# Issuing the loads of q, k and v three to four slots ahead, in a chunked retention and bilinear FFN kernel

## The chip, the cores and the metric

The kernel runs on one core of one Trainium2 chip. The metric is device time in microseconds (us) of one execution. A time is given as the median of several runs; a profile is of a single execution, which has a time of its own.

## The reference, cut to what matters

The attention part is a recurrence over 768 tokens for 4 batches and 8 heads of width 64; its output, as 3072 rows of 512, goes through a bilinear feed-forward layer.

```python
gamma = 1.0 - 2.0 ** (-5.0 - np.arange(H))
for t in range(S):
    state = gamma * state + einsum('bhd,bhe->bhde', k[:, :, t], v[:, :, t])
    y[:, :, t] = scale * einsum('bhd,bhde->bhe', q[:, :, t], state)
x = y.transpose(0, 2, 1, 3).reshape(B * S, H * D)      # 3072 x 512
out = ((x @ w_a) * (x @ w_b)) @ w_out                  # 512 -> 1536 -> 512
```

q, k and v are float32 in device memory, laid out as batch, head, token, width. The output is float32, 3072 by 512.

## The kernel before

**Slots.** The 3072 tokens are cut into 24 slots of 128 tokens; slot t is chunk t mod 6 of batch t div 6. The first six slots have a path of their own (`casts2`, `flip2`, `scores2`). The change concerns slots 6 to 23.

**The way of one slot.** Slots go in pairs, an even slot and the odd one after it. (1) *Load*: `load_slot` (line 106) issues from SyncE (SP) one transfer of 256 KB for k and one for v of each slot, and `load_two` (line 126) one of 512 KB for q of the whole pair. They fill float32 buffers `kf`, `qf`, `vf`, one for a pair, of which the pool `raw` has three each (line 58). A row of k or v is 64 floats, so a transfer of k or v is made of pieces of 256 bytes; q takes two tokens a piece, 512 bytes. (2) *Casts*: `casts(t)` (line 290) multiplies k and q by the decay tables into the bf16 tile `kqb` (two operations on GpSimd, POOL), and casts v into `vb`, on POOL too, but for slots 12 to 19, whose cast `v_cast` runs on ScalarE (ACT). (3) *Flip*: `flip(t)` (line 300) issues from SP a DMA transpose of `kqb` into the slot's half of the pair's `kqT`. (4) *Turn*: `turn(new, old)` (line 392) puts a pair's work on TensorE (PE): the state update from `kqb` and `vb`, then the scores of both slots (`scores`, line 325, which read both halves of `kqT`), and later the two parts of the output `y`, which ACT copies into `xt`.

**The feed-forward part.** Groups of slots J (`TILES`) run `ffn_a` and `ffn_g` (lines 517, 531) for 12 column blocks, VectorE (DVE) multiplying the two into `ht`. The output product (`Group`, line 620) is a seven-product scheme: its left operands are sums of blocks of `ht`, called `hs` (`hsum`, line 599), made on DVE or POOL. For J = 3, `hsum(3, 3, ...)` and two rounds of `hsums(3, ...)` are put on POOL between `casts(14)`, `casts(15)` and `casts(16)`. The last group of eight slots (`big`, line 851) uses such a scheme for the first two products too, with weight sums `wsa`, `wsb` that POOL makes (`weight_pieces`, line 736), after which POOL also multiplies some `ht` blocks there.

**What sets the order.** The helper `seq` (line 95) chains every instruction to the one before it on its engine, so each engine runs its work in the order in which the Python program writes it. This holds for SP too: all loads, transposes and stores are issued by SP, one after the other, onto one hardware DMA queue, and an SP instruction that waits holds up everything after it. `casts(t)` ends with the flip of slot t and then the loads of slot t + 2 (lines 296 to 298); `casts_two(6)` does slots 6 and 7 at once and then loads slots 8 and 9 (line 315). The list `LOADS` (line 21) gives the loads issued early, the last of which, "s6", is slots 6 and 7. `LATE_Q` (line 20) holds q of the pairs 14 and 18 back until the odd slot's loads.

The program order on POOL of the stretch that matters: casts of 6 and 7, 8, 9, 10, 11, `hs` of J = 2 around casts of 12 and 13, casts of 14, `hs`, casts of 15, `hs`, 16, 17, `hs`, 18, `hs`, 19, 20, 21, six weight pieces, 22, 23. On PE the turns that take in a new pair are, in order, those of pairs 6, 8, 10, 12, 14, 16, 18, 20 and 22.

Of the kernel before, what the change touches and what calls it, by code (L numbers as in the profile page):

```python
# [16 lines left out]
PAIRS = 3  # L17


LATE_Q = {14, 18}  # L20
LOADS = "p0 p1 w0 w1 a1 b1 a2 k2 q2 b2 v2 o0 o1 o2 o3 o4 o5 s6".split()


@with_exitstack
def kernel(
# [19 lines left out]
    NSLOT = B * NCH  # L45
# [49 lines left out]
    def seq(bi):  # L95
        ins = bi.ins
        prev = last.get(ins.engine)
        if prev is not None:
            tc.add_manual_dep(ins, prev.name, nosync, reason="program order")
        last[ins.engine] = ins  # L100
        return bi
# [3 lines left out]

    def load_slot(t, names="kqv"):
        b, ci = divmod(t, NCH)
        if t - 1 in LATE_Q:
            load_two("q", q, b, ci // 2, t - 1)
        for nm in names:  # L110
            src = {"k": k, "q": q, "v": v}[nm]
            if nm == "q":
                if t % 2 == 0 and t not in LATE_Q:
                    load_two(nm, src, b, ci // 2, t)
                continue
            if t % 2 == 0:
                whole[nm] = raw.tile([P, 2, H, D], F32, tag=nm + "f", name=nm + "f")
            raws[nm, t] = whole[nm][:, t % 2]
            s = src[b, :, ci * P : (ci + 1) * P, :].rearrange("h p d -> p h d")
            seq(nc.sync.dma_start(out=raws[nm, t], in_=s))  # L120

    def load_slots(t):
        for u, names in ((t, "kq"), (t + 1, "k"), (t, "v"), (t + 1, "v")):
            load_slot(u, names)

    def load_two(nm, src, b, u, t):
        f = raw.tile([P, H, 2, D], F32, tag=nm + "f", name=nm + "f")
        s = src[b, :, 2 * u * P : 2 * (u + 1) * P, :].rearrange("h (p two) d -> p h two d", two=2)
        seq(nc.sync.dma_start(out=f, in_=s))  # L129
        for par in range(2):  # L130
            raws[nm, t + par] = f[:, :, par, :]
# [25 lines left out]

    pending = list(LOADS)

# [78 lines left out]
    def cast(engine, dst, src):  # L238
        if engine is nc.scalar:
            seq(nc.scalar.copy(dst, src))  # L240
        else:
            seq(engine.tensor_copy(dst, src))  # L242
# [29 lines left out]
    def scaled(eng, t, i):  # L272
        tab = tabs[0] if i else tabs[1 if t < 2 * PAIRS else 2]
        dst, src, tab = kqb[t][:, i], raws["kq"[i], t], tab[:, t % NCH]
        if t < 2 * PAIRS:
            dst, src = (x.rearrange("p (hp r) d -> p hp r d", r=2) if x is src else x
                        for x in (dst, src))
            tab = tab.rearrange("p (hp r) o -> p hp r o", r=2).to_broadcast([P, HP, 2, D])
        else:
            dst = dst.rearrange("p hp r d -> p r hp d")  # L280
            src = src.rearrange("p (r hp) d -> p r hp d", r=2)
            tab = tab.rearrange("p (r hp) o -> p r hp o", r=2).to_broadcast([P, 2, HP, D])
        seq(eng.tensor_tensor(dst, src, tab, op=ALU.mult))  # L283

    def new_nat(t):
        kqb[t] = nat.tile([P, 2, HP, 2, D], BF16, tag="kqb", name="kqb")
        kb[t], qb[t] = kqb[t][:, 0], kqb[t][:, 1]
        vb[t] = nat.tile([P, H, D], BF16, tag="vb", name="vb")

    def casts(t):  # L290
        new_nat(t)
        scaled(nc.gpsimd, t, 0)
        scaled(nc.gpsimd, t, 1)
        if t not in range(12, 20):
            cast(nc.gpsimd, vb[t], raws["v", t])
        flip(t)
        if t + 2 < NSLOT:
            load_slot(t + 2)

    def flip(t):  # L300
        if t % 2 == 0:
            kqT[t // 2] = tra.tile([P, 2, 2, HP, P], BF16, tag="kqT", name="kqT", bufs=3)
        seq(nc.sync.dma_start_transpose(
            out=kqT[t // 2][:, t % 2].rearrange("p a b c -> p (a b) c"),
            in_=kqb[t].rearrange("p a hp r d -> p (a hp r d)")))

    def casts_two(t):
        for u in (t, t + 1):
            new_nat(u)
            scaled(nc.gpsimd, u, 0)  # L310
            scaled(nc.gpsimd, u, 1)
            flip(u)
        for u in (t, t + 1):
            cast(nc.gpsimd, vb[u], raws["v", u])
        load_slots(t + 2)

    def half(i):
        return slice(64 * i, 64 * i + 64)
# [660 lines left out]
    for ft in range(NFT):  # L979
        ffn_ab(1, ft)  # L980
    casts_two(6)
    ffn_out(0, 0, 0)
    weight_sum(3)
# [4 lines left out]
    ffn_out(0, 1, 1)  # L988
    weight_sum(4)
    casts(8)  # L990
    ffn_out(0, 2, 0)
    ffn_out(0, 2, 1)
# [3 lines left out]
    ffn_out(0, 3, 0)  # L996
    ffn_out(0, 3, 1)
    casts(9)
    turn(None, 6)
    single(1, AT0, AT1, FF)  # L1000
    casts(10)
    casts(11)
    blocks(2, 3, 6)
# [98 lines left out]
```

## Time and profile before

| | us |
|---|---|
| median of 3 runs | 222.13 (222.07 to 222.4) |
| the profiled execution | 222.79 |
| its span, first to last instruction of the program | 221.1 |
| DVE busy | 138.0 |
| ACT busy | 99.3 |
| POOL busy | 141.2 |

The DMA queue that SP feeds (q1 on the page) had packets for 75.8% of the time of 16 DMA engines. The page lists 18 transfers of k, 18 of v at 256 KB each and 12 of q at 512 KB as the large groups of loads; 18 DMA transposes took a median of 4.2 us from issue to landing.

How to read it: the profiled execution took 222.79 us, 1.7 us more than its span, which lie around the program's instructions, and 0.66 us more than the median of the runs. Busy time of an engine says nothing of where it waits; the timelines of the engines, in us from the span's start, and the view of waits (who waited for whom, in total, times, longest) tell that. In a timeline a row is: start, duration, engine, line, operation, output and inputs, shapes, count, and in brackets the idle time of the engine before it and what ended it. SPq is SP's queue of DMA issues; a row of it is the time for which SP was busy issuing, not the transfer, whose landing another view gives.

### The profile page before, as it was taken

How to read it: one execution, taken by the hardware profiler on the slowest of the kernel's cores; microseconds unless marked ns; L12 is line 12 of the kernel's file. 1: busy time of each engine (PE TensorE's matmuls, PEld its weight loads, DVE VectorE, ACT ScalarE, POOL GpSimd, SP SyncE). 2: the span in 40 equal slices, each digit the busy share in tenths (PEclk: the TensorE clock that was granted, in tenths of full speed). 3: DMA queues.
4: the chain of work that ended last, by engine and by line, in shares of the span. 5: the costliest groups of instructions: out<-in, count | busy, mean ns of one | idle time of the engine just before them, and what ended most of it. 6: DMA issues, size and time to landing. Idle time of an engine off the chain costs nothing.

```text
span 221.1 us, 5640 instructions
## 1 busy us (share of the span) xinstructions
PE 212.3 (96%) x2242; PEld 143.3 (65%) x2242; DVE 138.0 (62%) x254; ACT 99.3 (45%) x217; POOL 141.2 (64%) x163
## 2 busy tenths in 40 slices
PE   6789999999999999998999999999999999999994
PEld 2467445687468888887888565456865444448883
DVE  3776356846393463774377246986595777789642
ACT  3255325342243453453475345445545656542331
POOL 5265876775364659349782976999999996520000
PEclk9999999999999999999999999999999999999999
DMA  6999999998999999869999999990022000000054
GB/s 167 290 323 367 382 313 361 374 235 152 251 193 291 207 236 220 180 143 190 271 181 247 225 147 227 246 175 3 4 80 110 0 1 3 0 0 1 27 190 166
DMA packets 85146, 39.68 MB, mean 179 GB/s; under 512 B 57472, under 2 KB 78848, under 8 KB 85120
## 3 DMA queue, kind: packets, MB, share of 16 engines
q1 hardware_dynamic: 84976, 39.26, 75.8%
q8 instruction: 17, 0.28, 0.6%
q10 hardware_dynamic: 144, 0.07, 0.1%
q14 instruction: 9, 0.07, 0.1%
HBM read 28.31 MB, written 6.29 MB: 157 GB/s over the span
## 4 chain that ended last, share of the span: by engine, by line
PE 87%; SPq 4%; DMA 4%; POOL 2%; issue 1%; DVE 1%; ACT 0%; DVEq 0%
PE a L525 19%; PE g L537 18%; PE mA L641 12%; PE uA L781 8%; PE mB L641 6%; PE o L562 5%; PE uB L781 4%; DMA wstb<-in_moe_w_b_dram 4%; SPq L129 3%; PE mC L641 3%; PE at L330 2%; PE y L378 2%; PE uC L781 2%; PE st L348 2%; POOL hs L575 2%; PE ka L840 2%
## 5 line engine op out<-in xcount | busy, mean ns | idle before, releaser
L539 DVE TENSOR_TENSOR ht<-g,asb 128x256 bf16<-128x256 f32 (+1 forms) x74 | 36.9, 502 | 38.4 <-PE g L537 33.8
L525 PE MATMUL a<-xt,wa_bf 128*128 128x256 bf16 (+1 forms) x296 | 52.4, 305 | 0.2
L537 PE MATMUL g<-xt,wb_bf 128*128 128x256 bf16 (+1 forms) x296 | 52.2, 304 | 0.2 <-POOL wb_bf L242 0.2
L528 ACT CAST asb<-a 128x256 bf16<-128x256 f32 (+1 forms) x74 | 32.3, 437 | 39.0 <-PE a L525 36.6
L537 PEld LDWEIGHTS <-wb_bf 128*128 128x128 bf16 x296 | 28.6, 98 | 12.8 <-POOL wb_bf L242 0.3
L525 PEld LDWEIGHTS <-wa_bf 128*128 128x128 bf16 x296 | 27.9, 98 | 12.5 <-POOL wa_bf L242 0.4
L283 POOL TENSOR_TENSOR kqb<-kf,ktab 128x512 bf16<-128x512 f32 x22 | 23.0, 1051 | 16.6 <-DMA kf<-in_k_dram 14.9
L283 POOL TENSOR_TENSOR kqb<-qf,qtab 128x512 bf16<-128x512 f32 x18 | 19.0, 1053 | 12.8 <-DMA qf<-in_q_dram 12.8
L641 PEld LDWEIGHTS <-hs 128*128 128x128 bf16 x240 | 23.1, 98 | 5.6 <-POOL hs L575 1.7
L787 ACT COPY snap<-uA 128x512 f32<-128x512 f32 x30 | 16.7, 588 | 13.1 <-PE uA L781 13.1
L336 DVE TENSOR_TENSOR aT<-at,mask 128x512 bf16<-128x512 f32 x36 | 22.3, 681 | 0.3
L648 ACT COPY snaps<-mA 128x256 f32<-128x256 f32 x30 | 11.2, 374 | 21.2 <-PE mA L641 21.2
L641 PEld LDWEIGHTS <-ht 128*128 128x128 bf16 x180 | 17.5, 98 | 2.8
L575 POOL TENSOR_TENSOR hs<-ht,hs 128x384 bf16<-128x384 bf16 (+1 forms) x17 | 16.5, 982 | 2.5 <-DVE ht L539 2.5
L641 PE MATMUL mA<-wsum,hs 128*128 128x256 bf16 x120 | 16.1, 273 | 1.1 <-POOL hs L575 1.1
L575 POOL TENSOR_TENSOR ht<-gsb,asb 128x512 bf16<-128x512 bf16 x12 | 13.5, 1159 | 4.5 <-DVE gsb L575 4.5
L242 POOL CAST vb<-vf 128x512 bf16<-128x512 f32 x16 | 10.1, 645 | 8.4 <-DMA vf<-in_v_dram 8.2
L575 DVE TENSOR_TENSOR osb<-mB,snaps 128x256 f32<-128x256 f32 x20 | 8.4, 422 | 9.1 <-PE mB L641 4.7
L575 POOL TENSOR_TENSOR hs<-ht 128x384 bf16<-128x384 bf16 (+2 forms) x12 | 13.8, 1153 | 0.0
L389 ACT CAST xt<-y 128x512 bf16<-128x512 f32 x18 | 9.7, 589 | 2.3 <-PE y L378 2.2
L562 PE MATMUL o<-wo_bf,ht 128*128 128x512 bf16 x48 | 10.7, 379 | 0.0
L575 DVE TENSOR_TENSOR gsb<-uB,snap 128x512 bf16<-128x512 f32 x10 | 6.9, 685 | 5.4 <-ACT snap L787 2.6
(104 smaller groups left out, 325.9 us busy)
## 6 DMA issues: line engine op xcount, KB each, us to landing
qf<-in_q_dram SPq DMA_DIRECT2D x12, 512.0 KB, 5.9
out_dram<-osb SPq DMA_DIRECT2D x21, 256.0 KB, 4.2
kf<-in_k_dram SPq DMA_DIRECT2D x18, 256.0 KB, 4.6
vf<-in_v_dram SPq DMA_DIRECT2D x18, 256.0 KB, 5.3
wsta<-in_moe_w_a_dram SPq DMA_DIRECT2D x6, 512.0 KB, 7.9
wstb<-in_moe_w_b_dram SPq DMA_DIRECT2D x6, 512.0 KB, 8.2
wsto<-in_moe_w_out_dram SPq DMA_DIRECT2D x6, 512.0 KB, 8.7
kf<-in_k_dram SPq DMA_DIRECT2D x3, 512.0 KB, 7.2
```

Of the source, the lines that this page charges most:

```text
L283: seq(eng.tensor_tensor(dst, src, tab, op=ALU.mult))
L336: seq(nc.vector.tensor_tensor(aT[t][:, r], at[r], mask.to_broadcast([P, HP, P]), op=ALU.mult))
L525: seq(nc.tensor.matmul(a, wa_bf[:, kt, fs], xcols(J, kt, c0, c1), start=(kt == 0), stop=(kt == KT - 1)))
L528: seq(nc.scalar.copy(asb, a))
L537: seq(nc.tensor.matmul(g, wb_bf[:, kt, fs], xcols(J, kt, c0, c1), start=(kt == 0), stop=(kt == KT - 1)))
L539: seq(nc.vector.tensor_tensor(ht[J][:, ft, c0:c1], g, asbs.pop((J, ft, c0)), op=ALU.mult))
L562: seq(nc.tensor.matmul(o, ht[J][:, ft, i * P : (i + 1) * P], wo_bf[:, ft], start=(ft == 0), stop=(ft == NFT - 1), skip_group_check=True))
L575: seq(eng.tensor_tensor(dst, x, y, op=op))
L641: seq(nc.tensor.matmul(m, w, right[:, j], start=(first and j == 0), stop=(j == NP - 1), skip_group_check=True))
L648: seq(nc.scalar.copy(self.snaps[:, n], self.bank["A"]))
L781: seq(nc.tensor.matmul(m, w, right[:, k], start=(first and k == 0), stop=(k == 1), skip_group_check=True))
L787: seq(nc.scalar.copy(self.snaps[n], self.bank["A"]))
```

## The change

Loads move ahead. The pair 8 is loaded right after the pair 6, ahead of the transposes of 6 and 7. After that the loads that follow a flip are those of a slot four later in place of two, up to slot 17. The loads of 18 and 19 follow the flip of 15, those of 20 and 21 the flip of 18, those of 22 and 23 the flip of 19. q of a pair always goes with its even slot, so `LATE_Q` is gone.

```diff
-LATE_Q = {14, 18}
-LOADS = "p0 p1 w0 w1 a1 b1 a2 k2 q2 b2 v2 o0 o1 o2 o3 o4 o5 s6".split()
+LOADS = "p0 p1 w0 w1 a1 b1 a2 k2 q2 b2 v2 o0 o1 o2 o3 o4 o5 s6 s8".split()
+AHEAD = {8: (12,), 9: (13,), 10: (14,), 11: (15,), 12: (16,), 13: (17,), 15: (18, 19),
+         18: (20, 21), 19: (22, 23)}
 def load_slot(t, names="kqv"):
     b, ci = divmod(t, NCH)
-    if t - 1 in LATE_Q:
-        load_two("q", q, b, ci // 2, t - 1)
...
-            if t % 2 == 0 and t not in LATE_Q:
+            if t % 2 == 0:
 def casts(t):
...
-        if t + 2 < NSLOT:
-            load_slot(t + 2)
+        for u in AHEAD.get(t, ()):
+            load_slot(u)
 def casts_two(t):
...
-        load_slots(t + 2)
+        load_slots(t + 4)
```

The instructions of PE, DVE, ACT and POOL and their order are the same in both kernels. Only the order of SP's queue differs; the same transfers are in it. With k, q, v for the parts of a pair's loads, T for a transpose and "out" for a store of 256 KB, SP's queue from the loads of pair 6 to the transpose of slot 13 is:

```
before: k6 q6 k7 v6 v7 | T6 T7 k8 q8 k9 v8 v9 out T8 k10 q10 v10 out out T9 k11 v11 out T10
        k12 q12 v12 T11 k13 v13 out out T12 k14 v14 T13 | q14 k15 v15 T14 ...
after:  k6 q6 k7 v6 v7 | k8 q8 k9 v8 v9 T6 T7 k10 q10 k11 v10 v11 out T8 k12 q12 v12 out out T9
        k13 v13 out T10 k14 q14 v14 T11 k15 v15 out out T12 k16 q16 v16 T13 | k17 v17 T14 ...
```

(q8 holds q of slots 8 and 9, and so on.)

## The prediction

> **What bounds the kernel now.** First the page: busy times, slices, the chain.
>
> ```profile
> span 221.1 us, 5640 instructions
> PE 212.3 (96%) x2242; PEld 143.3 (65%) x2242; DVE 138.0 (62%) x254; ACT 99.3 (45%) x217; POOL 141.2 (64%) x163
> ...
> DMA  6999999998999999869999999990022000000054
> ...
> PE 87%; SPq 4%; DMA 4%; POOL 2%; issue 1%; DVE 1%; ACT 0%; DVEq 0%
> ```
>
> PE sets the time: 96% busy and 87% of the chain that ended last. A load that lands earlier is worth only the PE idle time that it takes away. But the DMA row is at 9 almost as long as slots are loaded, up to slice 27 (149 us), so loads, transposes and stores compete there.
>
> Next the view of waits: POOL's with the loads, then PE's own with engines that this change can reach.
>
> ```profile
> POOL kqb L283 <- DMA kf<-in_k_dram: 14.9, 9, 3.8
> POOL kqb L283 <- DMA qf<-in_q_dram: 12.8, 5, 5.6
> ...
> PE mA L641 <- POOL hs L575: 1.1, 1, 1.1
> ```
>
> POOL waits 27.7 us for k and q; PE waits for POOL's sums 1.1 us, once. The reader is to see the ratio: most of POOL's waiting reaches nobody. The timelines of PE and PEld place these waits, and give the times at which PE first reads the transposes of a pair (L330, `scores`):
>
> ```profile
> 60.97 0.64 PE L330 MATMUL at<-kqT 64*64 64x128 bf16 x32
> ...
> 76.36 0.64 PE L330 MATMUL at<-kqT 64*64 64x128 bf16 x32
> ...
> 97.54 0.64 PE L330 MATMUL at<-kqT 64*64 64x128 bf16 x32
> ...
> 105.26 0.50 PE L641 MATMUL mA<-wsum,hs 128*128 128x256 bf16 x3 [1.07 <-POOL hs L575]
> 124.98 0.22 PEld L641 LDWEIGHTS <-hs 128*128 128x128 bf16 x3 [0.31 <-POOL hs L575]
> 179.44 0.59 PE L781 MATMUL uB<-xs,wsa 128*128 128x512 bf16 x2 [0.30 <-DVE asb L575]
> ```
>
> **What the change can take away.** Rows of POOL's timeline, then two of DVE's:
>
> ```profile
> 97.08 1.04 POOL L283 TENSOR_TENSOR kqb<-qf,qtab 128x512 bf16<-128x512 f32 x1 [5.58 <-DMA qf<-in_q_dram]
> 103.42 1.78 POOL L575 TENSOR_TENSOR hs<-ht,hs 128x384 bf16<-128x384 bf16 x2
> 120.41 1.04 POOL L283 TENSOR_TENSOR kqb<-qf,qtab 128x512 bf16<-128x512 f32 x1 [5.06 <-DMA qf<-in_q_dram]
> 134.47 1.04 POOL L283 TENSOR_TENSOR kqb<-kf,ktab 128x512 bf16<-128x512 f32 x1 [3.25 <-DMA kf<-in_k_dram]
> ...
> 101.13 0.42 DVE L539 TENSOR_TENSOR ht<-g,asb 128x256 bf16<-128x256 f32 x1 [0.30 <-PE g L537]
> 178.09 0.69 DVE L575 TENSOR_TENSOR gsb<-uB,snap 128x512 bf16<-128x512 f32 x1 [2.11 <-POOL ht L575]
> ```
>
> - The stall at 105.26. POOL stands still 5.58 us for q of 14, then runs without a gap and ends the `hs` that PE wants at 105.2 (103.42 + 1.78), where PE wanted it at 104.19 (105.26 - 1.07). With q14 issued ahead of T11 it is there in time. The last `ht` block which that `hs` reads is ready at 101.55 (101.13 + 0.42); one operation of 0.9 us (half of 1.78) then ends near 102.5, 1.7 us ahead of need. The stall goes: **1.1 us**.
> - The weight load at 124.98 waits 0.31 for the next such sum, behind the wait of 5.06 us for q of 18. That goes too: **0.2 us** (bounds 0 and 0.31, since weight loads partly overlap PE).
> - The wait of 3.25 us at 134.47 goes, since k21 now follows T18 and not T19. POOL then comes up to 3 us sooner to the `ht` product for which DVE waits 2.11 us at 178.09, and PE at 179.44: **0.3 us** (bounds 0 and 0.3).
>
> Sum of the gain: **1.6 us**, bounds 1.1 and 1.7. What is late next on PE without these is not POOL; it is what PE reads from DMA.
>
> **What it adds: work ahead of the transposes.** No transfer is added, but each T that PE waits for now has more of them in front of it in SP's one queue. From issue to landing, three transposes before (T7, T9, T13, one instruction each):
>
> ```profile
> L303 SPq DMA_TRANSPOSE kqT<-kqb x1: 1233/1233/1233, 52.3 to 52.3; - x1
> DMA to landing us min/median/max: 3.2/3.2/3.2
> ...
> L303 SPq DMA_TRANSPOSE kqT<-kqb x1: 2133/2133/2133, 66.9 to 66.9; - x1
> DMA to landing us min/median/max: 5.0/5.0/5.0
> ...
> L303 SPq DMA_TRANSPOSE kqT<-kqb x1: 1237/1237/1237, 89.6 to 89.6; - x1
> DMA to landing us min/median/max: 3.1/3.1/3.1
> ```
>
> They land at 55.5, 71.9 and 92.7: 5.5, 4.5 and 4.8 us before PE reads them (60.97, 76.36, 97.54). The second has loads and stores in flight before it and takes 1.8 us longer than the other two: a transpose stands behind what was issued before. [...]
>
> What the queue moves, by windows (the last two numbers are DMA share and GB/s):
>
> ```profile
> 52.30:57.00 4.70, 4.70 (x27) 2.37 (x26) 4.25 (x10) 0.96 (x2) 1.05 (x2) 1.00 0.83 159
> 57.00:85.30 28.30, 28.30 (x344) 21.45 (x343) 14.62 (x30) 11.17 (x27) 17.52 (x19) 1.00 1.22 240
> 85.30:92.70 7.40, 7.40 (x102) 6.34 (x101) 3.82 (x10) 2.96 (x8) 5.28 (x6) 1.00 0.84 169
> 74.60:76.00 1.40, 1.40 (x15) 1.18 (x12) 0.79 (x2) 0.59 (x2) 1.40 (x2) 1.00 1.23 37
> ```
>
> From 57.0 to 85.3 it was full, at 240 GB/s over all kinds of transfer. In the stretches around it ran at 159 and 169, so 1.6 us of 4.7 (1 - 159/240) and 2.2 us of 7.4 lay open. The row at 74.6 is a hold in a transpose: share 1.23 but 37 GB/s for 1.4 us; I take one such hold of 1.2 us more as the upper case for each of T9 and T13, none as the lower.
>
> - **T7** gets the five loads of pair 8 in front: 1.5 MB (4 x 256 KB + 512 KB) or 1.57 million bytes, 6.5 us at 240 GB/s, less the 1.6 us open: 55.5 + 4.9 = 60.4, in time for 60.97 (60.4 to 62.0 if the gap can't be filled). No cost.
> - **T9** gets k11, v11, k12, q12, v12 more, the same bytes: 71.9 + 6.5 - 1.6 = 76.8, or 78.0 with a hold. PE wants it at 76.36: 0.4 to 1.6 late.
> - **T13** gets k15, v15, k16, v16 and, two at 512 KB, q14 and q16: 2.10 million bytes, 8.7 us, less 3.8 open: 92.7 + 4.9 = 97.6, or 98.8 with a hold, against 97.54: 0.1 to 1.3 late; 2.3 more if the second opening isn't filled.
>
> PE runs in order, so a late T stops all of PE. Behind the scores stand the turn and the feed-forward blocks; nothing else fills the hole. Lateness doesn't add up, since a stop at T9 moves the need for T13 back too: the cost is the larger of the two. The middles are 1.0 and 0.7; I take **1.5 us**, since the larger of two uncertain numbers lies above either middle, and since both sums count on openings that are filled to the last; bounds 0 and 3.6. After T13 the need is looser: the next turn came at 112 us, and POOL, which keeps its lead, no longer holds SP.
>
> Other edits come at nothing. The buffers: the third of each is free, since the pair three before has been cast when the load's turn comes; for v of 18, 20, 22 ACT casts it (`v_cast`) before the flip that SP must pass anyway. Merging q of 14 and 18 with the even slot moves 512 KB each and is in the sums. If a buffer's wait did show, it would hold SP's queue with the same price as a late T.
>
> **The sum**, against the profiled execution (222.79, span 221.1 and 1.7 around it): 222.79 - 1.6 + 1.5 = 222.7. The median of the runs is 0.66 lower, 222.13, so the forecast on that scale is **222.0**: no change that can be told, since 0.2% (0.44 us) is about what a measurement of this kernel tells apart.
>
> **The rivals.**
>
> - *Transposes in time, faster.* If the queue fills its open 3.8 us and no hold falls on T9 or T13, the lateness is 0.4 or less and the gain stays: 222.13 - 1.6 + 0.2 = 220.7. For it: the shares of 0.83 and 0.84 show room. Against: the need is met to within tenths in two places. [...]
> - *Transposes later than the gain, slower.* The place is T13 (and T9 before it) at the head of a turn on PE; the price is each us of lateness one to one; it decides the sign from a lateness of 1.6 us. With both holds, or the second opening unfilled, T13 is 1.3 to 3.6 late, middle 2.7: 222.13 - 1.6 + 2.7 = 223.2. For it: share 1.22 over 28 us, and the hold in the row at 74.6. Against: after 85.3 the queue did have room.
> - *The stall stays.* If `hs` came late for another reason than q14, the cost stands without the gain: 222.13 + 1.5 = 223.6. Against it: POOL has no other gap before 103.42, and `ht` is ready at 101.55.
>
> **How the numbers follow.** Lateness decides: from 1.2 to 2.1 us with a gain of 1.6 is the forecast, within 0.2% either way (221.7 to 222.6); below it is the first rival, above it the second. Forecast 0.29; faster rival 0.31; slower rival 0.36; the stall stays 0.04. So faster 0.31, same 0.29, slower 0.40. Cases of both signs hold most of the chance, so the range spans them: from no lateness at all, 220.5 (222.13 - 1.6), to lateness 3.4, 223.9 (222.13 - 1.6 + 3.4), a little inside the upper bound of 3.6.
>
> **What would show it.** In the changed kernel POOL's rows after 80 us have no wait for q or k above 0.5 us, and the 1.07 us before `mA` at 105 is gone (else the gain is wrong). T13 takes 5 us or more from issue to landing and PE shows idle time before L330, released by the DMA of `kqT`, near 76 or 98 us (else the added cost is wrong). The DMA row stays full without a dip from slice 10 to slice 17. The forecast fails if idle time turns up before L330 near 61 us, or if SP waits for a buffer.

## The result, and the profile after

The changed kernel is **slower**: 223.81 us (median of 22 runs, 222.43 to 225.47) against 222.65 us for the kernel before on the same chip (22 runs, 221.81 to 223.94). The ratio is 1.0057, with an interval of 1.0034 to 1.0079. On the scale of the 222.13 us shown ahead of the prediction that is 223.4 us: the forecast of no change was wrong, the second rival (transposes later than the gain, 223.2) was right. The profiled execution took 224.07 us with a span of 222.4; before it was 222.79 and 221.1.

The page of the changed kernel, the same lines as before:

```profile
span 222.4 us, 5629 instructions
PE 212.2 (95%) x2231; PEld 143.7 (65%) x2242; DVE 139.5 (63%) x254; ACT 99.3 (45%) x217; POOL 141.6 (64%) x163
...
DMA  6999999999999999999998969900013000000054
...
PE 70%; DMA 14%; POOL 6%; SPq 4%; issue 2%; DVE 2%; ACT 0%; POOLq 0%; ACTq 0%
```

PE is as busy as before, so the 1.3 us that the span grew are idle time of PE. The DMA row has lost the dips that it had in the 10th, 17th and 18th slice, shows two new ones further on (the 22nd and 24th), and is done with the loads a slice sooner (a 0 in the 27th): the queue is filled earlier. And in the chain that ended last PE fell from 87 to 70%, while DMA rose from 4 to 14%: the chain now runs over the transposes and the loads in front of them.

The waits of POOL, then of PE (engine, line waited for: us in total, times, longest):

```profile
POOL kqb L282 <- DMA qf<-in_q_dram: 2.9, 3, 1.6
POOL kqb L282 <- DMA kf<-in_k_dram: 2.7, 4, 1.2
```

```profile
core 0 of [0], span 222.4 us
PE at L329 <- DMA kqT<-kqb: 3.0, 2, 1.8
```

POOL's 27.7 us of waiting for k and q are down to 5.6. In their place PE waits 3.0 us for transposes, where it waited for none before. PE's timeline shows where (line numbers are one lower in this kernel; L329 is the scores):

```profile
61.02 0.64 PE L329 MATMUL at<-kqT 64*64 64x128 bf16 x32
...
78.26 0.64 PE L329 MATMUL at<-kqT 64*64 64x128 bf16 x32 [1.79 <-DMA kqT<-kqb]
...
100.67 0.64 PE L329 MATMUL at<-kqT 64*64 64x128 bf16 x32 [1.22 <-DMA kqT<-kqb]
...
106.83 0.82 PE L640 MATMUL mA<-wsum,hs 128*128 128x256 bf16 x6
```

The six `mA` products that the stall of 1.07 us split into 3 and 3 (the second three at 105.26) run in one row; the waits of 0.31 and 0.30 us at 125 and 179 are gone too. But the scores of pairs 8 and 12 wait 1.79 and 1.22 us for the transposes T9 and T13. From issue to landing these two took:

```profile
L302 SPq DMA_TRANSPOSE kqT<-kqb x1: 1379/1379/1379, 72.3 to 72.3; - x1
DMA to landing us min/median/max: 5.9/5.9/5.9
...
L302 SPq DMA_TRANSPOSE kqT<-kqb x1: 4926/4926/4926, 93.5 to 93.5; - x1
DMA to landing us min/median/max: 7.1/7.1/7.1
```

T9 lands at 78.2 (before 71.9), T13 at 100.6 (before 92.7). Part of the delay lies ahead of the issue. POOL has the casts of slot 9 done at 65.9, but SP, still issuing the loads and stores in front, issues T9 at 72.3 (before 66.9). T13 is issued at 93.5 (before 89.6), when SP and the casts come free together. The windows of the changed kernel, last two numbers DMA share and GB/s, tell why:

```profile
52.30:57.00 4.70, 4.65 (x26) 2.39 (x26) 4.25 (x7) 0.96 (x2) 3.14 (x4) 1.00 1.10 239
57.00:85.30 28.30, 26.45 (x326) 19.81 (x326) 16.69 (x32) 10.79 (x26) 13.86 (x16) 1.00 1.18 233
85.30:92.70 7.40, 7.40 (x69) 6.39 (x67) 2.55 (x6) 2.92 (x8) 7.40 (x9) 1.00 1.22 230
92.70:100.60 7.90, 6.66 (x97) 5.50 (x96) 5.41 (x12) 3.69 (x10) 4.50 (x5) 1.00 1.24 191
97.40:99.40 2.00, 2.00 (x25) 1.58 (x22) 0.94 (x3) 1.27 (x4) 2.00 (x3) 1.00 0.93 19
75.60:77.00 1.40, 0.86 (x14) 0.50 (x12) 0.70 (x2) 0.74 (x2) 0.98 (x1) 1.00 1.14 43
```

Both openings are filled (239 for 159, 230 for 169 GB/s), as the prediction assumed. But the queue was held for 2.0 us at 19 GB/s up to 1.2 us before T13 landed, and for 1.4 us at 43 GB/s up to 1.2 us before T9 did.

### The profile page after: what moved, and what is told of

It is laid out like the page before. It is cut to its first block, busy times and chain, and to the rows that moved or that the text cites. A ratio compares the mean times of both kernels' runs of the same rounds, so it can differ in the third digit from the quotient of the medians.

```text
span 222.4 us, 5629 instructions
## 1 busy us (share of the span) xinstructions
PE 212.2 (95%) x2231; PEld 143.7 (65%) x2242; DVE 139.5 (63%) x254; ACT 99.3 (45%) x217; POOL 141.6 (64%) x163
## 4 chain that ended last, share of the span: by engine, by line
PE 70%; DMA 14%; POOL 6%; SPq 4%; issue 2%; DVE 2%; ACT 0%; POOLq 0%; ACTq 0%
PE a L524 12%; PE g L536 12%; PE mA L640 10%; PE uA L780 8%; DMA kqT<-kqb 6%; PE mB L640 5%; DMA qf<-in_q_dram 5%; PE o L561 5%; POOL kqb L282 4%; PE uB L780 4%; DMA wstb<-in_moe_w_b_dram 4%; SPq L128 3%; PE mC L640 3%; PE at L329 2%; PE uC L780 2%
## 5 line engine op out<-in xcount | busy, mean ns | idle before, releaser
L536 PEld LDWEIGHTS <-wb_bf 128*128 128x128 bf16 x296 | 28.6, 98 | 12.8 <-POOL wb_bf L241 0.3
L640 PEld LDWEIGHTS <-hs 128*128 128x128 bf16 x240 | 23.3, 98 | 3.9
L640 PEld LDWEIGHTS <-ht 128*128 128x128 bf16 x180 | 17.5, 98 | 2.8
L640 PE MATMUL mA<-wsum,hs 128*128 128x256 bf16 x120 | 15.7, 273 | 0.0
L239 ACT CAST gst<-st 128x256 bf16<-128x256 f32 x13 | 4.8, 372 | 11.1 <-PE st L347 11.1
```

The costliest lines, as they stand in the source:

```text
L536: seq(nc.tensor.matmul(g, wb_bf[:, kt, fs], xcols(J, kt, c0, c1), start=(kt == 0), stop=(kt == KT - 1)))
L640: seq(nc.tensor.matmul(m, w, right[:, j], start=(first and j == 0), stop=(j == NP - 1), skip_group_check=True))
```

## The experiments

**The theory**: the change is two things. POOL gets q in time, which takes away three stalls of PE (1.07 + 0.31 + 0.30 = 1.7 us); and the loads stand ahead of transposes that PE needs, which costs the lateness of the latest one. **Rivals**: something else that came with the lead slows PE; or the lateness of T9 and T13 adds up; or putting q of 14 and 18 with the even slot is what makes the transposes late.

Each experiment is a short edit of `AHEAD` in the changed kernel, or of `LATE_Q` in the kernel before. All were timed against the kernel before on the same chip; the ratios are to it.

**Both transposes relieved.** The loads of pair 12 go behind T9, those of pair 16 behind T13; the rest of the lead stays.

```diff
-AHEAD = {8: (12,), 9: (13,), 10: (14,), 11: (15,), 12: (16,), 13: (17,), 15: (18, 19),
+AHEAD = {9: (12, 13), 10: (14,), 11: (15,), 13: (16, 17), 15: (18, 19),
```

Expected:

> The loads of slot 12 come after the transpose of 9 in place of before it, and those of slot 16 after the transpose of 13; everything else is as in the changed kernel. Queue theory (the cost is the lateness of the transposes of 9 and 13 behind loads, 3.1 us in all; the gain of 1.9 us at 105, 125 and 179 us stays): both waits of PE at L329, 1.8 and 1.2 us, go, and the time is 1.9 us under the kernel before (ratio 0.9915). Rival (having more loads in flight slows the engines or the queue as a whole, and the waits are where it shows): only part comes back, ratio 0.998 or more.

Measured: 221.26 us, ratio 0.9932 (0.9907 to 0.9957), so the rival's 0.998 is out. T9 lands at 73.2, T13 at 96.4, and the waits at 78 and 100 us are gone. PE's waits and a row of its timeline:

```profile
core 0 of [0], span 220.2 us
PE at L329 <- DMA kqT<-kqb: 0.9, 1, 0.9
...
118.06 0.64 PE L329 MATMUL at<-kqT 64*64 64x128 bf16 x32 [0.93 <-DMA kqT<-kqb]
```

So the lateness of these two transposes is the whole loss, and the gain is real. What stays is a third late transpose, T17, which lands at 118.0. In the changed kernel it lands no earlier (118.2), but there PE comes later, at 120.19, and doesn't notice.

**One transpose relieved at a time.** T9 alone, then T13 alone:

```diff
-AHEAD = {8: (12,), 9: (13,), 10: (14,), 11: (15,), 12: (16,), 13: (17,), 15: (18, 19),
+AHEAD = {9: (12, 13), 10: (14,), 11: (15,), 12: (16,), 13: (17,), 15: (18, 19),
```

> Only the loads of slot 12 are moved behind the transpose of 9; the transpose of 13 still has those of slot 16 before it. Queue theory, with lateness that does not add up: the wait of 1.8 us near 78 us goes, but the queue up to the transpose of 13 holds the same transfers, so that one lands at the same 100.6 us and its wait grows from 1.2 to 3.1 us; the time stays that of the changed kernel (ratio 1.0055). Rival (each wait is a cost of its own): 1.8 us comes back, ratio 0.997.

Measured: 223.75 us, ratio 1.0066 (1.0039 to 1.0093). PE's waits:

```profile
core 0 of [0], span 222.1 us
PE at L329 <- DMA kqT<-kqb: 2.7, 1, 2.7
```

The wait at 78 us is gone, and the one at 100 us grew from 1.2 to 2.7 us: T13 lands at 100.3 all the same. Nothing was won by relieving T9 alone, so lateness doesn't add up. The later transpose sets the cost; an earlier stop only takes some of it in advance.

```diff
-AHEAD = {8: (12,), 9: (13,), 10: (14,), 11: (15,), 12: (16,), 13: (17,), 15: (18, 19),
+AHEAD = {8: (12,), 9: (13,), 10: (14,), 11: (15,), 13: (16, 17), 15: (18, 19),
```

> Only the loads of slot 16 are moved behind the transpose of 13. Queue theory: the wait near 78 us stays at 1.8 us, the transpose of 13 lands before PE wants it, and the time is that of the kernel before within 0.3 us (1.8 lost, 1.9 won; ratio 0.9995). Rival (waits cost one by one): 1.2 us back, the same ratio; so this run tells only whether the second wait goes by the order of the queue alone.

Measured: 223.29 us, ratio 1.0040 (1.0013 to 1.0068), which is above what was expected.

```profile
core 0 of [0], span 221.2 us
PE at L329 <- DMA kqT<-kqb: 1.8, 1, 1.8
```

The profile does what the theory says: T13 lands at 94.7 and isn't waited for, T9's 1.8 us stay, and the span is that of the kernel before. The median is higher because 4 of the 12 runs had a mean granted clock of 0.990 to 0.992, with 224.6 us in the middle; the 8 at 0.997 or more had 222.8, beside 222.55 for the kernel before. In the kernel before no run that was set beside it had less than 0.997.

**More in front of T9.** All of pair 12, the loads of slot 13 too, goes ahead of T9, and nothing more ahead of T13:

```diff
-AHEAD = {8: (12,), 9: (13,), 10: (14,), 11: (15,), 12: (16,), 13: (17,), 15: (18, 19),
+AHEAD = {8: (12, 13), 10: (14,), 11: (15,), 12: (16,), 13: (17,), 15: (18, 19),
```

> The loads of k and v of slot 13 (512 KB) are put ahead of the transpose of 9 as well. Queue theory: 512 KB at 240 GB/s is 2.2 us, so the transpose lands near 80.4 us, the wait near 78 us grows from 1.8 to about 4.0 us and takes in that of the transpose of 13, which has the same transfers before it as in the changed kernel; total lateness 4.0 against 3.1, ratio 1.0095. Rival (waits add up one by one): 4.0 + 1.2 - 1.9, ratio 1.015. No effect of the order: 1.0055.

Measured: 226.83 us, ratio 1.0179 (1.0145 to 1.0213), twice the loss expected. PE's waits, then the windows around the pause (the third number from the end is the granted clock):

```profile
core 0 of [0], span 224.7 us
PE at L329 <- DMA kqT<-kqb: 4.1, 1, 4.1
```

```profile
76.50:80.20 3.70, 0.01 (x2) 0.00 (x0) 0.30 (x1) 0.37 (x1) 1.21 (x1) 1.00 1.12 260
80.20:83.60 3.40, 2.97 (x48) 2.30 (x49) 2.29 (x4) 0.74 (x2) 0.00 (x0) 0.50 1.20 227
83.60:87.00 3.40, 3.40 (x56) 2.77 (x55) 1.47 (x4) 1.35 (x4) 1.22 (x2) 1.00 1.26 259
```

T9 lands at 80.6 and PE waits 4.1 us, both within 0.2 us of what was expected. By its time alone the run would be nearer the rival's 1.015, that waits add up; but the profile has this one wait only, and T13, which lands at 99.1, is not waited for (PE reads it at 103.06). What comes on top is the clock: in the 3.4 us from 80.2 TensorE runs at half clock, which is up to 1.5 us of work lost, half of the 2.97 us for which PE was busy there. The pause is paid for twice.

**All three relieved.** As the first experiment, with the loads of 18 and 19 behind T17 too:

```diff
-AHEAD = {8: (12,), 9: (13,), 10: (14,), 11: (15,), 12: (16,), 13: (17,), 15: (18, 19),
+AHEAD = {9: (12, 13), 10: (14,), 11: (15,), 13: (16, 17), 17: (18, 19),
```

> As the run with the loads of slots 12 and 16 moved back, and the loads of 18 and 19 follow the transpose of 17 in place of that of 15, since that run's profile has a new wait of 0.9 us at 118 us for the transpose of 17. Queue theory: that wait goes too and none of the waits for transposes is left, so the whole gain of 1.9 us shows: ratio 0.9915, 0.9 us under that run. Rival (loads in flight cost something of their own): ratio stays near 0.993.

Measured: 220.88 us, ratio 0.9918 (0.9896 to 0.994), span 219.3, and no wait for a transpose left in PE's view of waits. By the span, 1.8 us under that of before, the gain is kept whole. The interval of the ratio holds the rival's 0.993 too; what speaks for the theory here is the profile.

**Only q of 14 with its even slot**, and nothing of the lead, in the kernel before:

```diff
-LATE_Q = {14, 18}
+LATE_Q = {18}
```

> The kernel before with one edit: q of pair 14 is issued with slot 14, not with slot 15; all other loads two slots ahead. Theory (the gain at 105 us comes from q of 14 alone): the wait of POOL of 5.6 us and the stall of PE of 1.07 us go, the transpose of 13 has 512 KB more before it and still lands ahead of its need, and the time is 1.1 us lower, ratio 0.995; a wait of up to 0.5 us for the transpose of 17 may take its place in part. Rival (the whole lead is needed): the stall stays and the ratio is 1.000.

Measured: 221.06 us, ratio 0.9924 (0.9899 to 0.995); the expected 0.995 lies at the end of the interval. The profile has more gone than expected: the stalls at 125 and 179 us too, not only the one at 105, though q of 18 and k of 21 are loaded where they were. PE's timeline has the six `mA` in one row (L641 is the same line as L640 above):

```profile
103.87 0.82 PE L641 MATMUL mA<-wsum,hs 128*128 128x256 bf16 x6
```

**Both q with their even slot**, and nothing of the lead:

```diff
-LATE_Q = {14, 18}
+LATE_Q = set()
```

> The kernel before with both late loads of q, of 14 and of 18, issued with the even slot. Queue theory: q of 18 now stands before the transpose of 17, which landed at 117.2 and is wanted near 117.2 once the stall at 105 is gone; 512 KB more make it about 1.3 us late, which eats the gain of 1.1 to 1.4 us: ratio 1.000. Rival (a load issued earlier is never worse): ratio 0.994.

Measured: 220.92 us, ratio 0.9925 (0.9901 to 0.995), span 219.1. The theory as I had applied it here was wrong: I expected T17 to be late behind q18, and it wasn't. The rows of T16 and T17 in this kernel:

```profile
L303 SPq DMA_TRANSPOSE kqT<-kqb x1: 1237/1237/1237, 106.3 to 106.3; - x1
DMA to landing us min/median/max: 3.6/3.6/3.6
...
L303 SPq DMA_TRANSPOSE kqT<-kqb x1: 3039/3039/3039, 110.2 to 110.2; - x1
DMA to landing us min/median/max: 6.0/6.0/6.0
```

T17 does take 6.0 us behind q18, but it is issued at 110.2 (before 112.7), since POOL has its casts done sooner: its waits for q are 3.0 us, where they were 12.8. It lands at 116.2, and PE reads it at 117.0.

**The lead without the move of q**: the changed kernel, with q of 14 and 18 again with the odd slot.

```diff
+LATE_Q = {14, 18}
...
+        if t - 1 in LATE_Q:
+            load_two("q", q, b, ci // 2, t - 1)
...
-                if t % 2 == 0:
+                if t % 2 == 0 and t not in LATE_Q:
```

> The other half of the change by itself: the loads three to four slots ahead as in the changed kernel, but q of 14 and 18 again with the odd slot's loads. Theory (the gain is that POOL has q14 before it wants it, the cost is the bytes ahead of the transposes of 9 and 13): q14 is still issued ahead of the transpose of 11, now right ahead of k15, so POOL has it in time and the stalls of PE at 105, 125 and 179 us stay away; and the same bytes stand in front of the transpose of 13, so PE waits near 78 and 100 us for about 3 us in all, as in the changed kernel. Ratio 1.0055, between 1.002 and 1.009. Rival (issuing q with the even slot is what makes the transposes late): the wait near 100 us goes or falls below 0.3 us, ratio 1.000 or less.

Measured: 223.76 us, ratio 1.0055 (1.0027 to 1.0083), the same as the whole change. PE's waits and a window (granted clock third from the end):

```profile
core 0 of [0], span 222.8 us
PE at L332 <- DMA kqT<-kqb: 1.8, 1, 1.8
```

```profile
78.10:83.60 5.50, 5.26 (x68) 3.79 (x72) 3.22 (x6) 1.49 (x4) 0.00 (x0) 0.69 1.26 231
```

PE waits 1.8 us for T9. The wait near 100 us that was expected is missing in this profile, but not because T13 is early: it lands at 100.9. After the first pause the clock was 0.69 over 5.5 us, which is a loss of 1.7 us (5.5 x 0.31); PE came to the scores of pair 12 only at 101.1. So the lost clock took the place of the wait, and the rival is refuted by its time.

**All ten profiles together.** The span less what PE waits in it for POOL's sums and for transposes (for the kernel before this is 1.07 + 0.31 + 0.30, the three stalls of the theory):

| kernel | span | those waits of PE | difference |
|---|---|---|---|
| before | 221.1 | 1.7 | 219.4 |
| after | 222.4 | 3.0 | 219.4 |
| both transposes relieved | 220.2 | 0.9 | 219.3 |
| T9 relieved | 222.1 | 2.7 | 219.4 |
| T13 relieved | 221.2 | 1.8 | 219.4 |
| all three relieved | 219.3 | 0 | 219.3 |
| q of 14 only | 219.5 | 0 | 219.5 |
| both q only | 219.1 | 0 | 219.1 |
| lead only | 222.8 | 1.8 | 221.0 |
| more ahead of T9 | 224.7 | 4.1 | 220.6 |

Eight of ten leave 219.1 to 219.5. The last two leave 1.6 and 1.2 us more, and these are the profiles with a stretch of lower clock (0.69 over 5.5 us, 0.50 over 3.4 us). Beside the late transposes and the clock no cost of the change is to be seen. The best versions, all three relieved and the two with q alone, can't be told apart.

## Why the prediction was wrong

- **The gain: right.** 1.6 us were forecast for three stalls; all three went, for 1.7. The cause was named rightly for the large one: q of 14 by itself brings a ratio of 0.9924 (0.9899 to 0.995). For the two small ones, 0.2 and 0.3 us, I had named q of 18 and k of 21, and these needn't move: both stalls go with q of 14 alone. I had left 4 in 100 to the case that the stall would stay.
- **T7 at no cost: right**, by a hair. It lands at 61.0, where 60.4 was forecast, and PE reads it at 61.02 without a wait.
- **Lateness doesn't add up: right.** 1.79 + 1.22 = 3.0 us of waiting are the lateness of T13 alone: 100.6 against the need at 97.54 is 3.1. With T9 relieved the wait is one of 2.7.
- **The openings are filled: right.** 239 and 230 GB/s stand where 159 and 169 stood.
- **The failed step: "The middles are 1.0 and 0.7; I take 1.5 us".** The mechanism was right and the term too small: 3.0 us. T9 came 1.8 us late, where the sum gave 0.4 to 1.6, and T13 came 3.1 late, where it gave 0.1 to 1.3 (only the outer bound of 3.6 held it). For T13 the windows split the miss, which is the landing at 100.6 less the sum's 97.6, 3.0 us. Against the 240 GB/s of the sum, the stretches at 233, 230 and 191 GB/s lost 0.8, 0.3 and 1.6 us (28.3 x 7/240, 7.4 x 10/240, 7.9 x 49/240), 2.7 in all. In the last of them lies the hold of 2.0 us at 19 GB/s, which alone is 1.8 (2.0 x (1 - 19/240)), where the middle had half of 1.2. The sum took the 240 GB/s of before's full stretch as the rate all the way, and took one hold of a middling size as the upper case. I had "holds" as the exception for a transpose; they fell on both.
- **The weighing of the term.** Even the sum's best case had T13 0.1 us late, so a lower rate or a hold could only add to it. The slower rival took 2.7, and the measured 3.0 is within 0.3 of it. That is nearer than its own working: the middle of its 1.3 and 3.6 is 2.45, and 3.6 itself counts 2.3 for an opening that the windows had given as 2.2.
- **"After T13 the need is looser": right only while PE is late.** With T9 and T13 relieved, T17 is the next one that PE waits for, 0.93 us at 118.06.
- **Not in the sum: the clock.** Of the 22 runs of the changed kernel 7 had a mean granted clock of 0.990 to 0.992, with a median of 224.57 us; the others, at 0.997 or more, had 223.38. So the runs at full clock are 0.7 us over before in the median, and those with lost clock 1.2 us more. With the gain of 1.7 the lateness in the runs at full clock is an estimated 2.4 us (0.7 + 1.7), less than the 3.0 of the one run whose profile was kept. That the 3.0 less 1.7 of that profile, 1.3, comes so near to the difference of all medians, 1.2, is in part luck: the medians hold some lost clock in place of the longer pause.
- **Loads issued early.** In the changed kernel POOL's waits for k and q fell from 27.7 to 5.6 us. The kernel as a whole isn't faster for it: the lead alone gives a ratio of 1.0055 (1.0027 to 1.0083), since what is issued early stands ahead of a transfer that is needed sooner (T9 landed at 71.9 before, and at 78.2 in the changed kernel).

The gain needed none of the lead. One load, q of 14, was late for an engine that somebody waited for; moving it by one slot (ratio 0.9924) is worth as much as the best form of the whole change (0.9918, 0.9896 to 0.994). The rest of the lead took away waits of POOL that nobody felt.

## What to carry to other kernels

When loads share a queue with transfers that stand between two engines (here the transposes), issue a load ahead of such a transfer only if its own reader is on the path; work out the landing of each such transfer with the bytes put ahead of it, and leave room for a lower rate and for holds (here T13 came 3.0 us behind such a sum). Look for the one load behind the stall and move that alone. And price a pause of TensorE above its length: of the five profiles here with a pause of 1.8 us or more, two (1.8 and 4.1 us) have a lower clock behind it, which cost an estimated 1.2 to 1.7 us more.

## What the runs showed of the hardware

**A lower clock after pauses of 1.8 and 4.1 us.** In the profile with a pause of 4.1 us the clock of TensorE was 0.50 for 3.4 us, and 1.00 in the 3.4 us behind that. In that of the lead alone it fell behind a pause of 1.78 us: the 0.69 over 5.5 us shown above loses as much, 1.7 us, as 3.4 us at half clock do. A mean clock of 0.992 over 222 us is about one such stretch (222 x 0.008 = 1.8 us lost). Runs below 0.995 were 7 of 22 for the changed kernel, 4 of 12 each with T9 relieved, with T13 relieved and with the lead alone, and 5 of 6 with more ahead of T9; the profiles of these kernels show a longest pause of 1.8, 2.7, 1.8, 1.8 and 4.1 us. There were none in 24 runs of the four kernels whose longest such pause is 0.9 us or less, nor in the runs of before whose clock is on record (0.997 at the least). The length of a pause alone doesn't decide: the profiles with pauses of 1.8 us in the changed kernel and with T13 relieved, and the one with 2.7 us, keep the full clock behind them (1.00 over the 4.0 us from 78.0, 1.00 over the 3.5 us from 78.3, and 1.000 in the mean of the span). The pauses of the runs without a kept profile are not on record, so what pause brings the drop is not shown.

**Holds of the transposes.** In the profiles of the kernel before, the changed kernel and the one with T13 relieved there are stretches of 1.4 to 2.2 us in which the queue moves 19 to 44 GB/s though its engines are taken (a share of 0.93 to 1.38), while a transpose is under way. In the kernel before those at 74.6 and 99.8 begin 1.3 and 0.7 us, in the changed kernel those at 75.6 and 97.4 begin 1.9 and 0.7 us, after a transfer that the kernel doesn't issue: a packet of 16 KB on a queue marked "instruction". Ahead of the hold that began at 97.4 in the changed kernel, the view of DMA from 96.5 to 97.5 has (packets, MB, share; a packet's whole time counts where it starts, so long packets bring the share over 100%):

```profile
q1 hardware_dynamic: 818, 0.21, 356.4%
q8 instruction: 1, 0.02, 6.9%
```

Ahead of the hold at 99.8 in the kernel before, from 99 to 100:

```profile
q1 hardware_dynamic: 479, 0.12, 161.7%
q8 instruction: 1, 0.02, 9.0%
```

That one brings about the other was not tried, so it stays an association. If it does, it would explain why holds fall on other transposes when the work is moved; no run here shows that.
